# A dynamic convolution in front of a tanh-shrink layer: products in two tiles, softmax four superblocks ahead, one part of the products on VectorE, second sums from superblock 13 on

## The chip, the cores and the metric

The kernel runs on one core of a Trainium2 chip. A core has five engines that run beside each other, each with its own queue of instructions in order: TensorE (PE, matmuls; PEld is its loading of weights), VectorE (DVE), ScalarE (ACT), GpSimd (POOL) and SyncE (SP, which here only issues DMAs). GpSimd issues DMAs too. An instruction that waits for a semaphore holds up everything behind it on its engine. On-chip data lies in SBUF; matmuls write to PSUM, a small memory of eight banks. The metric is the time of one execution on the device in microseconds; lower is better.

## The reference

Cut to what is computed, with batch 8, sequence 4096, 192 channels, 8 heads of 24 channels and 7 taps, and a layer of 2048 hidden units:

```python
w = softmax(weight_gen, axis=-1)                 # per token, head: 7 weights
x_pad = np.concatenate([zeros(B, 6, D), x], axis=1)
x_unf = x_pad[:, idx, :].reshape(B, S, 7, 8, 24) # idx: the token and the six before it
out = np.einsum('bshk,bskhg->bshg', w, x_unf)    # sum over the 7 taps
h = out.reshape(B * S, D) @ w_in                 # 192 x 2048
g = h - np.tanh(h)
return g @ w_out                                 # 2048 x 192
```

All inputs and the output are float32.

## The kernel before

The 32768 tokens are cut into 32 superblocks (n = 0 to 31) of 1024 tokens, four to a sequence. Within one, partition p holds the eight tokens 8p to 8p + 7 (index j) and the six tokens ahead of them (the halo). A superblock goes through these steps:

- `load_x` and `load_wg` (SP's DMA queue) bring the tokens and the raw weights. Of x there are two tiles, of wg two. The first superblock of a sequence gets zeros over its halo by a further small DMA (L124).
- Softmax: `softmax_exp` on ScalarE (L147), two partial sums over the taps on VectorE (`softmax_sum`, L161), and at the end of a loop a reciprocal (L176) and a scaling (L207), both on VectorE with the reciprocals in a corner of a PSUM tile.
- `products`: GpSimd multiplies the tokens with the weights, one product tile per tap, all seven in one tile `pr` of 7 x 8 x 192 bfloat16 per partition (two such tiles, `ppool`). L236 is every such multiply; 1536 of its elements per partition are one tap.
- Sums by DMA: a DMA from GpSimd's queue that adds what it reads to what stands in its target (`dma_sum`, L214). The first sum adds taps 3, 4, 5 to 0, 1, 2, so that four tiles are left (6, 0, 1, 2). In the superblocks in `TWO_SUMS` a second sum adds 2 and 6 to 0 and 1, so that two are left. It's issued in `products` of the next superblock, behind that one's first multiply (`second_sum`). Superblocks 2 to 4 (`PART`) add only two taps and keep five tiles.
- Transposes (`conv_sums`, L311): matmuls with an identity turn the remaining tiles into channel-major form and add them up in PSUM; ScalarE copies the result out as `convT` (L337). Fewer tiles are fewer matmuls: each costs 48 (24 pairs) per superblock.
- `gemm1` (L354): 16 tiles f of hidden units, six matmuls each, in one of three PSUM tiles `ph`, which the transposes use as well. ScalarE computes the tanh (L367, `th`), VectorE the difference (L368, `gt`).
- `out_stream` (L389): the second matmul, as a stream of 128 small steps ("pairs") per superblock, running one superblock behind; ScalarE copies its results out (L408), and SP stores them (L412).

The order on every engine is written out by hand, in the order of the program. The loop over n has 16 steps f. At step f it issues `gemm1(n, f)`, and then what the plan names for this step: in `STEADY` and `FIRST`, `pairs` says how many steps of the output stream follow each f, `t2` and `t1` where the transposes of superblock n + 1 stand (f = 13 for two thirds of the channels and f = 14 for the last third), `sums` where VectorE's partial softmax sums stand, and `scale` where the scaling stands. At f = 1 come the exponential of n + 3 and `products(n + 2)`; at f = 7 the load of x for n + 3 (`X_AT`), held behind the last difference issued.

So loop n transposes n + 1, lets GpSimd work on n + 2, and makes the softmax of n + 3.

The softmax here doesn't subtract the row's maximum and nothing guards it: scores larger than these inputs give would overflow.

## Time and profile before

| what | before |
|---|---|
| time, median of 4 runs | 751.86 us (748.69 to 756.33) |
| time of the profiled execution | 751.58 us |
| its span, first to last instruction | 749.8 us |
| mean granted TensorE clock | 0.991 |
| L354 PE (gemm1), 3072 matmuls | 406.1 us busy |
| L389 PE (output stream), 7936 matmuls | 398.4 us busy |
| L311 PE (transposes), 2496 matmuls into pc | 49.9 us busy, 16.6 us idle before them |
| L368 DVE (difference), 512 | 603.3 us busy, mean 1219 ns |
| L367 ACT (tanh), 512 | 506.8 us busy, mean 1026 ns |
| L236 POOL (products), 95 | 629.8 us busy |
| L214 POOL (sums by DMA), 43 issues | 55.0 us busy |

"Busy" is the time in which at least one instruction of the group ran; instructions of one engine may overlap a little, so a sum of means can be over the busy time. "Idle before" is the time for which the engine stood still just ahead of the group, with the releaser that ended it. The lines by time give the start, the length, the engine, the line, the operation, the tile written and the tiles read, how many instructions are merged, and in brackets an idle time before it with its releaser. A DMA issue of GpSimd counts as busy for about 1.28 us; the data lands later.

### The profile page before, as it was taken

To read this page: it belongs to the slowest core of one execution; us is meant where nothing else is said; L and a number is where in the kernel's file an instruction comes from. 1 tells how busy PE (TensorE), PEld (TensorE's weight loads), DVE (VectorE), ACT (ScalarE), POOL (GpSimd) and SP (SyncE) were. 2 spreads that over 40 slices of the span, in tenths; PEclk is the share of its full clock that TensorE was granted. 3 is DMA by queue.
4 is the path that set the end of the run, shared out by engine and by line. 5 is a ranking of instruction groups with operands and counts; after the bars stand their busy time and mean duration, and the time that the engine had idled before them with its cause. 6 is when DMAs were issued, how large, how long until landed. Compare 5 with 4: busy or idle time off the path is not lost.

```text
span 749.8 us, 30497 instructions
## 1 busy us (share of the span) xinstructions
PE 723.4 (96%) x13928; PEld 564.5 (75%) x13928; DVE 664.6 (89%) x655; ACT 638.6 (85%) x872; POOL 668.7 (89%) x150
## 2 busy tenths in 40 slices
PE   3899999999999999999999999999999799999998
PEld 2477777777887777777777777777787577777777
DVE  7999889998889998999999999999989689998983
ACT  4888888888888888898989899898989588988883
POOL 7999999999999999999999999999999999999000
PEclk9899999999999999999999999999999899999999
DMA  8944536765655567785695787579668757673412
GB/s 233 245 104 114 171 115 167 192 181 126 178 154 170 171 177 158 200 192 167 193 233 143 185 209 179 170 198 210 166 173 184 186 153 183 184 178 84 112 44 87
DMA packets 32511, 124.99 MB, mean 167 GB/s; under 512 B 4495, under 2 KB 9343, under 8 KB 28414
## 3 DMA queue, kind: packets, MB, share of 16 engines
q0 software_dynamic: 17664, 46.01, 35.8%
q1 hardware_dynamic: 14718, 77.03, 27.6%
q8 instruction: 109, 1.79, 0.9%
q14 instruction: 20, 0.16, 0.1%
HBM read 54.52 MB, written 25.17 MB: 106 GB/s over the span
## 4 chain that ended last, share of the span: by engine, by line
PE 84%; DMA 5%; POOL 4%; DVE 4%; ACT 1%; issue 1%; SPq 0%; DVEq 0%; POOLq 0%
PE obank L389 39%; PE ph L354 39%; DMA pr<-pr 4%; PE pc L311 4%; POOL pr L236 4%; DVE gt L368 2%; PE po L432 1%; DVE pr L236 1%; DMA x_t<-zero 1%; ACT th L367 1%; ACT convT L337 0%; DVE wsm L207 0%; PE obank L311 0%; SPq L114 0%; POOL pr L214 0%
## 5 line engine op out<-in xcount | busy, mean ns | idle before, releaser
L368 DVE TENSOR_TENSOR gt<-ph,th 128x1024 bf16<-128x1024 f32 x512 | 603.3, 1219 | 65.3 <-ACT th L367 64.9
L236 POOL TENSOR_TENSOR pr<-x_t,wsm 128x3072 bf16<-128x3072 f32 (+3 forms) x95 | 629.8, 6830 | 7.0 <-PE obank L389 5.9
L367 ACT ACTIVATE th<-ph 128x1024 f32<-128x1024 f32 x512 | 506.8, 1026 | 70.5 <-PE ph L354 66.2
L354 PE MATMUL ph<-convT,w_in 64*128 64x512 bf16 x3072 | 406.1, 379 | 5.9 <-DVE gt L368 3.5
L389 PEld LDWEIGHTS <-gt 64*128 64x128 bf16 x7936 | 351.8, 94 | 73.7 <-issue 11.1
L389 PE MATMUL obank<-w_out,gt 64*128 64x192 bf16 x7936 | 398.4, 243 | 0.2 <-issue 0.2
L354 PEld LDWEIGHTS <-w_in 64*128 64x128 bf16 x3072 | 169.9, 95 | 83.6 <-issue 12.0
L408 ACT ACTIVATE out_sb<-obank 128x192 f32<-128x192 f32 x248 | 82.3, 332 | 12.7 <-PE obank L389 10.1
L214 POOL DMA_DIRECT2D pr<-pr x43 | 55.0, 1280 | 20.3 <-DMA pr<-pr 10.7
L311 PEld LDWEIGHTS <-pr 64*128 64x128 bf16 x2664 | 51.0, 101 | 24.1 <-POOL pr L236 10.4
L311 PE MATMUL pc<-ident,pr 64*128 64x64 bf16 x2496 | 49.9, 193 | 16.6 <-POOL pr L236 10.3
L337 ACT ACTIVATE convT<-pc 128x1024 bf16<-128x1024 f32 (+1 forms) x62 | 50.5, 816 | 6.8 <-PE pc L311 6.3
L161 DVE TENSOR_REDUCE zsum<-e_t 128x32 f32<-128x224 f32 (+1 forms) x61 | 23.7, 388 | 2.8 <-ACT e_t L147 2.8
L147 ACT ACTIVATE e_t<-wg_t 128x448 f32<-128x448 f32 x32 | 18.2, 569 | 7.6 <-DMA wg_t<-in_weight_gen_dram 7.6
L207 DVE TENSOR_TENSOR wsm<-e_t,pc 128x448 f32<-128x448 f32 x28 | 17.4, 621 | 3.3 <-DVE pc L176 0.5
L176 DVE RECIPROCAL pc<-zsum 128x64 f32<-128x64 f32 x28 | 15.4, 551 | 0.0
L432 PE MATMUL po<-w_out,gt 64*128 64x192 bf16 x256 | 11.2, 243 | 0.0
L236 DVE TENSOR_TENSOR pr<-x_t,obank 128x1536 bf16<-128x1536 f32 (+4 forms) x8 | 10.4, 1350 | 0.8 <-ACT wsm L199 0.6
L432 PEld LDWEIGHTS <-gt 64*128 64x128 bf16 x256 | 10.8, 93 | 0.0
L446 DVE TENSOR_TENSOR out_sb<-po,ot 128x192 f32<-128x192 f32 x8 | 2.9, 358 | 9.0 <-ACT ot L445 9.0
L445 ACT ACTIVATE ot<-po 128x192 f32<-128x192 f32 x8 | 2.6, 331 | 7.3 <-PE po L432 7.3
L467 POOL DMA_DIRECT2D w_in<-in_moe_w_in_dram x4 | 2.4, 627 | 2.8 <-ACT e_t L147 2.8
(19 smaller groups left out, 18.3 us busy)
## 6 DMA issues: line engine op xcount, KB each, us to landing
x_t<-in_x_dram SPq DMA_DIRECT2D x31, 1344.0 KB, 6.0
pr<-pr POOLq DMA_DIRECT2D x27, 1152.0 KB, 9.9
out_dram<-out_sb SPq DMA_DIRECT2D x31, 768.0 KB, 3.8
pr<-pr POOLq DMA_DIRECT2D x16, 768.0 KB, 6.7
wg_t<-in_weight_gen_dram SPq DMA_DIRECT2D x32, 224.0 KB, 6.8
x_t<-in_x_dram SPq DMA_DIRECT2D x1, 768.0 KB
w_out<-in_moe_w_out_dram POOLq DMA_DIRECT2D x1, 768.0 KB, 9.6
out_dram<-out_sb SPq DMA_DIRECT2D x4, 192.0 KB, 4.0
```

What stands on the lines that cost most here:

```text
L147: last_exp[0] = nc.scalar.activation(out=e_t[:].rearrange("p j h k -> p (j h k)"), in_=wg_t[:].rearrange("p j h k -> p (j h k)"), func=ACT ...
L161: nc.vector.reduce_sum(out=zsum_of[n][:, j0 * H : j1 * H], in_=e_of[n][:, j0:j1].rearrange("p j h k -> p (j h) k"), axis=AX.X,)
L214: nc.gpsimd.dma_start(out=pr[:, k0:k1].rearrange("p k j d -> p k (j d)"), in_=pr[:, src0:src1:step].rearrange("p k j d -> p k (j d)"), acc ...
L236: return eng.tensor_mul(pr[:, k0:k1, j0:j1, :].rearrange("p k j (h g) -> p k (j h) g", h=H), bass.AP(tensor=x_v.tensor, offset=x_v.offset ...
L311: nc.tensor.matmul(pc[r][:, col : col + R] if home else pc[:, r, col : col + R], lhsT=prods[c][gi][r * R : (r + 1) * R, 2 * j : 2 * j + 2] ...
L337: last_conv[0] = nc.scalar.activation(out=out, in_=pc[:, :, 0:cols].rearrange("p r (cj t) -> p r cj t", t=R), func=ACT.Copy,)
L354: nc.tensor.matmul(ph[:, r, :], lhsT=w_in[r * R : (r + 1) * R, c, f * P : (f + 1) * P], rhs=convT[r * R : (r + 1) * R, c, :], start=(c == ...
L367: last_act[0] = nc.scalar.activation(out=th[:], in_=ph_f, func=ACT.Tanh)
L368: last_sub[0] = nc.vector.tensor_sub(gt[:], ph_f, th[:])
L389: mm = nc.tensor.matmul(po[:, 0:D], lhsT=g_of[n][f][r * R : (r + 1) * R, col : col + P], rhs=w_out[r * R : (r + 1) * R, f, :], start=(r == ...
L408: last_act[0] = nc.scalar.activation(out=out_sb[:, j, :], in_=po[:, 0:D], func=ACT.Copy)
L432: nc.tensor.matmul(po[:, r, 0:D], lhsT=g_of[n][f][r * R : (r + 1) * R, col : col + P], rhs=w_out[r * R : (r + 1) * R, f, :], start=(f == 0 ...
```

## The change

- The products lie in two tiles: `pa` with taps 0 to 3 (three buffers) and `pb` with taps 4 to 6 (one buffer). GpSimd multiplies taps 0 and 1, taps 2 and 3, and taps 4 to 6. The first sum adds all of `pb` to taps 0 to 2 and stands behind the last multiply; the second sum adds taps 2 and 3 to 0 and 1 and stands in the next superblock's products behind its second multiply.
- For superblocks from 4 on (`HELP`), GpSimd's first multiply leaves out the last of the eight tokens; VectorE makes these two taps of that token at f = 3 of the loop, by a copy of 16 weights to the PSUM tile of that f and a multiply of 384 elements. `products` returns `rest`, which holds this and the remaining GpSimd work and is called at f = 3.
- `TWO_SUMS` holds all superblocks from 13 on (19 instead of 13).
- The softmax runs four superblocks ahead from loop 4 on (loop 4 makes two); the exponential is computed in place, with three tiles of raw weights and four of softmax results.
- `load_x` of n + 3 stands at f = 1, held behind GpSimd's first multiply of n + 2. The first superblock of a sequence is loaded without its halo in the first partition, in three DMAs and the zeros.
- The product of superblock 1 is cut differently, with two tiles in place of `pb` out of the output's pool. The plans `STEADY` differ in `pairs` and `sums`.

```diff
-    TWO_SUMS = tuple([n for n in range(13,NTOT) if n%3])
-    SUM_FIRST = tuple(range(5,32))
+    KA, KH = 4, 2
+    TWO_SUMS = (13, 14, 15, 16, 17, 18, 19, 20, 21, 22, 23, 24, 25, 26, 27, 28, 29, 30, 31)
+    AHEAD = 4
+    HELP_AT = 3
...
-    wgpool = ctx.enter_context(tc.tile_pool(name="wgpool", bufs=2))
-    ppool = ctx.enter_context(tc.tile_pool(name="ppool", bufs=2))
+    wgpool = ctx.enter_context(tc.tile_pool(name="wgpool", bufs=3))
+    papool = ctx.enter_context(tc.tile_pool(name="papool", bufs=3))
+    pbpool = ctx.enter_context(tc.tile_pool(name="pbpool", bufs=1))
+    wspool = ctx.enter_context(tc.tile_pool(name="wspool", bufs=4))
...
-            mul(nc.gpsimd, 0, 2)
-            second_sum(n - 1)
-            mul(nc.gpsimd, 2, 6)
-            if n in SUM_FIRST:
-                dma_sum(pr, 0, 3, 3, 6)
-            mul(nc.gpsimd, 6, K)
...
+        x_after[n + 1] = mul(nc.gpsimd, 0, KH, 0, J - 1 if n in HELP else J)
+        mul(nc.gpsimd, KH, KA)
+        second_sum(n - 1)
+
+        def rest(ph=None):
+            if n in HELP:
+
+                w = ph[:, 0, 0 : KH * H].rearrange("p (k h) -> p k h", k=KH)
+                nc.vector.tensor_copy(w, wsm[:, J - 1].rearrange("p h k -> p k h")[:, 0:KH])
+                nc.vector.tensor_mul(
+                    pa[:, 0:KH, J - 1, :].rearrange("p k (h g) -> p k h g", h=H),
...
+                    w.rearrange("p k (h o) -> p k h o", o=1).to_broadcast([P, KH, H, G]),
+                )
+            if n in PART:
+                dma_sum(pa[:, 0:2], pa[:, 2:4])
+            mul(nc.gpsimd, KA, K)
...
+                dma_sum(pa[:, 0:3], pb[:, 0:3])
...
     def second_sum(n):
 
         if n in to_sum:
-            dma_sum(to_sum.pop(n), 0, 2, 2, K, 4)
+            pa = to_sum.pop(n)
+            dma_sum(pa[:, 0:2], pa[:, 2:4])
...
-        taps=[(V, 0, 1, 0, J), (V, 1, 2, 0, J), (G_, 2, 5, 0, J), (G_, 5, 7, 0, J)],
+        taps=[(V, 0, 1, 0, J), (V, 1, 2, 0, J), (G_, 4, 6, 0, J), (G_, 6, 7, 0, J), (G_, 2, 4, 0, J)],
...
-    STEADY = dict(pairs=(4, 12, 0, 16, 0, 16, 0, 16, 0, 6, 10, 6, 10, 8, 8, 16), t1=(14, 8), t2=(13, 0), scale=14, sums=(2, 5))
+    STEADY = dict(pairs=(5, 11, 0, 16, 4, 12, 6, 10, 0, 6, 10, 8, 8, 8, 8, 16), t1=(14, 8), t2=(13, 0), scale=14, sums=(1, 13))
...
+        soft = [m for m in (n + 3,) * (n <= AHEAD) + (n + 4,) * (n >= AHEAD) if m < NTOT]
         for f in range(NFT):
-            gemm1(n, f)
+            ph = gemm1(n, f)
...
-            if f == X_AT and n + 3 < NTOT:
-                load_x(n + 3, last_sub[0])
+            if f == (9 if n == 1 else HELP_AT) and n + 2 < NTOT:
+                rest(ph)
+            if f == (9 if n == 1 else 1):
+                emit_x(n + 3)
+                if soft and n != AHEAD and soft[0] + 1 < NTOT and n > 1:
+                    load_wg(soft[0] + 1)
```

`emit_x(m)` calls `load_x(m, x_after[m])`.

## The prediction, made before the change was run

> **What bounds the kernel now.** I read the page's busy shares first, then the chain of waits, then single loops of the steady part, then the one place where TensorE stands still.
>
> ```profile
> PE 723.4 (96%) x13928; PEld 564.5 (75%) x13928; DVE 664.6 (89%) x655; ACT 638.6 (85%) x872; POOL 668.7 (89%) x150
> PE 84%; DMA 5%; POOL 4%; DVE 4%; ACT 1%; issue 1%; SPq 0%; DVEq 0%; POOLq 0%
> ```
>
> TensorE is busy for 96% and carries 84% of the chain; the 5% of DMA and 4% of POOL in it are one place, shown below. VectorE and GpSimd are at 89% each, so a cut on TensorE is worth something only while both still keep up. Two whole loops, one whose transposes take four product tiles per token block (n = 5 to 12 and every third later), one with two (both sums made):
>
> ```profile
> 130.10:152.50 22.40, 22.40 (x454) 17.61 (x451) 20.36 (x21) 19.83 (x27) 22.10 (x5) 1.00 0.60 162
> 505.69:527.41 21.72, 21.72 (x403) 16.83 (x400) 20.29 (x20) 19.59 (x28) 21.42 (x6) 1.00 0.86 213
> ```
>
> The columns are the stretch, its length, then PE, PEld, DVE, ACT and POOL busy, granted clock, DMA share. TensorE has no gap at full clock in either: 22.40 us is its own length with four tiles, 21.72 us with two. VectorE leaves 2.04 and 1.43 us free. GpSimd's own pace is in its timeline:
>
> ```profile
> 112.11 1.28 POOL L214 DMA_DIRECT2D pr<-pr  x1 [0.30 <-POOL pr L236]
> 112.93 19.99 POOL L236 TENSOR_TENSOR pr<-x_t,wsm 128x1536 bf16<-128x1536 f32 x3
> 133.22 1.30 POOL L214 DMA_DIRECT2D pr<-pr  x1 [0.30 <-POOL pr L236]
> ...
> 373.04 1.28 POOL L214 DMA_DIRECT2D pr<-pr  x1 [0.30 <-POOL pr L236]
> 373.86 8.97 POOL L236 TENSOR_TENSOR pr<-x_t,wsm 128x1536 bf16<-128x1536 f32 x2
> 382.75 1.26 POOL L214 DMA_DIRECT2D pr<-pr  x1
> 383.53 11.59 POOL L236 TENSOR_TENSOR pr<-x_t,wsm 128x6144 bf16<-128x6144 f32 x1
> 395.42 1.28 POOL L214 DMA_DIRECT2D pr<-pr  x1 [0.30 <-POOL pr L236]
> ```
>
> From one first sum to the next: 133.22 - 112.11 = 21.11 us with one sum, 395.42 - 373.04 = 22.38 us with two. So GpSimd gains 1.3 us on TensorE per one-sum superblock and loses 0.7 us or more per two-sum one (more where it also waits for the first sum to land, up to 1.53 us). The debt comes due here:
>
> ```profile
> 584.95 1.22 POOL L214 DMA_DIRECT2D pr<-pr  x1 [1.28 <-DMA pr<-pr]
> ```
> ```profile
> 596.33 1.04 PE L311 MATMUL pc<-ident,pr 64*128 64x64 bf16 x32 [5.58 <-DMA pr<-pr]
> 597.16 1.49 PE L389 MATMUL obank<-w_out,gt 64*128 64x192 bf16 x16
> 598.42 1.51 PE L354 MATMUL ph<-convT,w_in 64*128 64x512 bf16 x6
> 599.70 1.16 PE L389 MATMUL obank<-w_out,gt 64*128 64x192 bf16 x16
> 600.68 0.41 PE L311 MATMUL pc<-ident,pr 64*128 64x64 bf16 x16
> ```
>
> The second sum of superblock 26, issued at 584.95, is awaited by its transposes: TensorE idles 5.58 us. The four groups after it take 4.35 us from start to start (596.33 to 600.68), where the same four took 2.44 us one loop of this kind earlier (502.58 to 505.02). The stall costs 5.58 + 1.91 = 7.5 us.
>
> **The change, part by part.**
>
> Transposes. Superblocks 15, 18, 21, 24, 27 and 30 go from four tiles to two. The two transposes of a superblock take 0.93 + 0.46 us with four (starts 123.95 to 124.88, 126.85 to 127.31) and 0.47 + 0.23 us with two (502.58 to 503.05, 505.02 to 505.25): 0.69 us less, six times, 4.1 us. All of it lies on the path, as TensorE has no gap there.
>
> GpSimd. The multiplies become 2688, 3072 and 4608 wide instead of 3072, 6144 and 1536: three as before, 384 fewer elements. Rows of the ramp give 2.90, 5.62 and 8.33 us for 1536, 3072 and 4608, so 1.77 ns per element, and 0.68 us less per superblock from n = 4. The new paces are 20.43 us with one sum and 21.70 us with two, against 22.40 and 21.72 of TensorE: the debt stops growing. The wait before the second sum goes too: it now stands behind two multiplies, 11.8 us after the first sum's issue (0.8 + 0.45 + 4.94 + 5.58, the 0.45 being what a multiply loses while a sum is issued), and in before it could start 10.4 to 11.4 us after it wherever it waited.
>
> GpSimd's head start. The second sum stands one multiply later than before, so superblock n needs its first sum issued about 18.5 us before its transposes (11.8 plus a median 6.7 to land). The ramp reaches the first sum of n = 5 at 113.9 us (112.11; +0.2 for product 1 cut in three; -0.68 for n = 4; +2.25 because the sum now comes behind the last tap: 8.33 + 5.58 + 4.94 against 11.02 + 5.58 after the previous tap group). Its transposes start at 123.95 with a tile that needs no sum, and that sum landed 9.8 us after issue: 0 to 1 us of stall, I take 0.3. By n = 13 GpSimd is at 113.9 + 8 x 20.43 = 277.3; the transposes are due at 280.93 + 22.40 = 303.3; that leaves 7.5 us, kept to the end at equal pace. The 7.5 us stall goes, and what is late next is nothing of GpSimd's.
>
> The single second product tile (the three last taps of n + 1 wait for the sum of n to land, 8.8 to 12.1 us, 11.8 covered): at most 0.3 us of GpSimd, inside the head start. Softmax four ahead and three first tiles remove the waits "POOL pr <- PE obank" (5.9 us over five places, all off TensorE's path): nothing for the end, if they came back they'd cost head start.
>
> SP's queue. The load of x(n+3) moves to f = 1 and waits for GpSimd's first multiply of n + 2. Behind it stand one weight load and one store of the output. In the ramp that multiply ends near 79 us, so the weights of 6 land near 86.5, about when their exponential is due in loop 3 (84.1 + 2.8): 0 to 1 us, I take 0.2. Later the multiply is done before the queue gets there. The extra loads at a sequence start replace one load and an overwrite; they land long before use.
>
> VectorE. 28 superblocks (n = 4 to 31, in loops 2 to 29) get a copy of 16 elements and a multiply of 384, right behind the subtraction of f = 3, in order before that of f = 4. The multiply has a row: 128x384 took 547 ns. The copy has none: reciprocals of 32 and 64 elements took 343 and 551 ns, so their fixed part is 135 ns, and products of 192 and 384 (356, 547 ns) give 165 ns; I take 0.18 us, bounds 0.13 and 0.34. Two waits of VectorE on itself, as between reciprocal and scale (0.10 us): together 0.85 us after the 0.08 by which neighbours overlap, between 0.75 and 1.1. VectorE then needs 21.14 of 21.72 us. Who waits: the next subtraction, and the matmuls of f = 6, which take the PSUM tile that the copy writes. In the loop at 507 us the subtraction of f = 3 ends at 514.4, about 0.3 earlier once the partial sum at f = 2 has moved to f = 1 (there 0.26 us were idle); the help ends at 515.0 and the matmuls of f = 6 start at 515.09. The later subtractions are met the same way, since the partial sum of f = 5 goes to f = 13 (0.60 us idle behind it) and the pairs now spread the matmuls of f = 4 to 7. So it just fits, with under 0.1 us to spare; I take 0.05 us per loop, 1.4 us. Loop 4 makes two softmaxes: 0.75 + 0.55 + 0.62 more on VectorE against about 1.2 us free, 0.6 us.
>
> A rule that speaks against it: the Trainium skill, "GPSIMD Engine Reference", Key points, says that GpSimd shares its SBUF interfaces with VectorE and suffers from VectorE instructions with two SBUF inputs. No VectorE row here has two SBUF inputs beside a GpSimd multiply, and the new one reads its weights from PSUM, so by the rule nothing is added. Were it to count all the same, GpSimd would stand still for the 0.55 us of that row, 10 us over the last 19 superblocks, 3 us of it past the head start (an estimate).
>
> Sum: 749.8 - 4.1 - 7.5 + 0.3 + 0.2 + 1.4 + 0.6 = 740.7 (the 0.2 of product 1 is covered: its transposes start 1.3 us after its last multiply). The profiled execution's time is 1.8 us above its span (751.58), and the median 0.3 above that: 742.8. The small costs may be zero (740.3). I forecast 742.
>
> **The rivals.**
>
> VectorE's help is dearer than it fits (1.1 to 1.3 us instead of 0.85): TensorE waits 0.2 to 0.4 us in each of 28 loops, 747 to 752. For: the margin worked out above is under 0.1 us. Against: VectorE's total still leaves time, and three tiles of tanh and PSUM take up jitter.
>
> GpSimd gains nothing: the 2688 multiply, cut out of each tap's row, costs as much as 3072 (5.62 us). Then the first sum of 13 comes at 114.6 + 8 x 21.11 = 283.5, the head start is 0.6 us, and 18 superblocks lose 0.66 us each: 11.3 us of stall, 753. Against: the rows at four widths lie on one line.
>
> Slower: the help lands wholly on TensorE's path, as VectorE's one in-order queue holds the subtraction of f = 4 and the PSUM tile of f = 6. Below about 0.9 us it hides; from 1.6 us on TensorE loses 0.7 us or more in 28 loops, 20 us: 760 and above. For: no row shows such a pair beside GpSimd's wide multiplies, and it waits twice for VectorE itself. Against: the 384 row.
>
> That the change does not do what it says: the instruction order shows both sums of 13 to 31, so this is excluded; TensorE's odd gap such as the 0.96 us at 290, put down to "issue", may stay.
>
> **How the numbers follow.** The four runs of before spread over 1.0% (748.69 to 756.33), so 1% is what can be told from no change: 744.3 and 759.4. Forecast 0.57 (738 to 746, a tenth of it above 744.3), dear help 0.14, GpSimd unchanged 0.09, slower 0.17, other small stalls 0.03. Faster 0.51, same 0.32, slower 0.17. The range 738 to 758 leaves out the slower case and a little below.
>
> **What would show it.** Right: no TensorE wait over 1 us on a sum past 300 us; loops of 21.7 us from 300 to 700; GpSimd at 20.4 and 21.7 us from first sum to first sum; the copy and multiply 0.7 to 0.9 us together. Wrong: waits of the f = 6 or f = 7 matmuls on VectorE in every loop (second or fourth case), or the 2688 multiply near 5.6 us (third). A TensorE wait near 124 us over 1 us would mean that the single second tile or the later sum of the ramp costs more than I gave it.

## The result, and the profile after

| what | before | after |
|---|---|---|
| time, median | 753.04 us (64 runs, 744.84 to 756.36) | 755.59 us (43 runs, 753.00 to 760.48) |
| profiled execution, its span | 751.58, 749.8 us | 756.84, 755.1 us |

The ratio on record is 1.005, with a 95% interval of 1.0037 to 1.0062 (that of the two medians is 1.003): a little slower, and inside the 1% that the prediction counted as no change. The forecast of 742 us is missed by 14 us. Between the spans of the profiled executions, the prediction's sum had 9.1 us of gain (749.8 to 740.7); 5.3 us were lost.

First the page of the changed kernel, busy shares and chain:

```profile
PE 723.6 (96%) x13640; PEld 560.2 (74%) x13640; DVE 685.4 (91%) x711; ACT 640.7 (85%) x872; POOL 656.9 (87%) x157
PE 93%; DVE 3%; issue 2%; ACT 1%; DMA 0%
```

TensorE issues 288 matmuls fewer and is as long busy as before (723.6 to 723.4 us). The chain has lost its 5% of DMA and its 4% of GpSimd, as forecast, and "issue" has gone from 1% to 2%. Whole stretches tell where the time went; each line is the stretch and its length, the busy time of PE, PEld, DVE, ACT and POOL, the granted clock, the DMA share and GB/s. Before, from the transposes of superblock 4 to those of 13, and from there to those of 31:

```profile
101.20:304.70 203.50, 202.54 (x4058) 161.16 (x4056) 183.39 (x181) 178.97 (x243) 199.09 (x38) 1.00 0.62 165
304.70:708.20 403.50, 397.62 (x7491) 309.80 (x7489) 363.76 (x355) 354.13 (x485) 373.57 (x83) 0.99 0.71 177
```

After, the same work:

```profile
102.00:316.30 214.30, 204.06 (x4059) 161.94 (x4057) 191.57 (x203) 180.24 (x245) 202.54 (x42) 1.00 0.70 172
316.30:712.70 396.40, 394.55 (x7204) 304.68 (x7202) 375.04 (x386) 354.65 (x484) 357.31 (x85) 1.00 0.78 188
```

From superblock 13 on the change gains 7.1 us. Before that, where it takes nothing from TensorE, the same instructions take 10.8 us longer, 9.3 of them with TensorE idle (214.30 - 204.06 against 203.50 - 202.54). With 0.8 us lost at each end that is the 5.3 us. What TensorE waits for in the early part is in its timeline; the brackets hold the idle time before the line and its releaser:

```profile
107.00 0.45 PE L336 MATMUL pc<-ident,pb 64*128 64x64 bf16 x19 [1.57 <-issue]
...
133.45 0.57 PE L415 MATMUL obank<-w_out,gt 64*128 64x192 bf16 x9 [1.55 <-issue]
...
155.70 0.32 PE L415 MATMUL obank<-w_out,gt 64*128 64x192 bf16 x3 [1.65 <-issue]
...
227.86 0.57 PE L415 MATMUL obank<-w_out,gt 64*128 64x192 bf16 x9 [2.42 <-issue]
...
250.10 0.32 PE L415 MATMUL obank<-w_out,gt 64*128 64x192 bf16 x3 [1.37 <-issue]
...
276.38 0.57 PE L415 MATMUL obank<-w_out,gt 64*128 64x192 bf16 x9 [1.42 <-issue]
```

Six stretches, 10.0 us, each in or shortly after the transposes of superblocks 4, 5, 6, 9, 10 and 11. No semaphore event ends them: their operands are there. A stretch breaks off in the middle of a run of equal matmuls (the 16 of one group stand as 7 and 9). GpSimd's own lines show that it is not late:

```profile
136.66 1.30 POOL L219 DMA_DIRECT2D pa<-pb  x1 [0.30 <-POOL pb L253]
...
157.11 1.28 POOL L219 DMA_DIRECT2D pa<-pb  x1 [0.30 <-POOL pb L253]
...
385.87 9.33 POOL L253 TENSOR_TENSOR pb<-x_t,wsm 128x4608 bf16<-128x4608 f32 x1
395.50 1.28 POOL L219 DMA_DIRECT2D pa<-pb  x1 [0.30 <-POOL pb L253]
396.32 11.01 POOL L253 TENSOR_TENSOR pa<-x_t,wsm 128x2688 bf16<-128x2688 f32 x2
406.79 1.72 POOL L219 DMA_DIRECT2D pa<-pa  x1
407.57 9.32 POOL L253 TENSOR_TENSOR pb<-x_t,wsm 128x4608 bf16<-128x4608 f32 x1
417.28 1.28 POOL L219 DMA_DIRECT2D pa<-pb  x1 [0.39 <-POOL pb L253]
```

395.50 to 417.28 is 21.78 us from first sum to first sum with two sums (21.70 forecast); with one sum it is 20.45 (136.66 to 157.11; 20.43 forecast). No transposes wait for a sum any more.

**What an "issue" stretch is.** The page's queues list one that is neither a sum nor a load of data; after, and its row before:

```profile
q0 software_dynamic: 19296, 50.73, 39.1%
q1 hardware_dynamic: 15040, 77.00, 29.9%
q8 instruction: 106, 1.74, 0.9%
```
```profile
q8 instruction: 109, 1.79, 0.9%
```

The columns are packets, MB and share of the engines' time. 1.74 MB in 106 packets are 16.4 KB each; and TensorE has 2 x 13640 = 27280 instructions (matmuls and weight loads), 256 times 106.6. Before, the row says 109 and its 27856 instructions are 256 times 108.8. So each packet is a block of 256 instructions of TensorE, which comes through the same DMA engines as the data. Counted in TensorE's instructions, block i starts to load when TensorE is about 182 past 256 i if the DMA engines are free, and later if they are busy. From the DMA records of all 18 kernels (1668 such loads between 80 and 720 us), by how far TensorE was past 256 i when the load began (its few waits for semaphores counted too), with the longest pause between two TensorE starts around it or in the 1.5 us behind it:

```
past 256 i     loads   with a pause over 0.45 us   mean pause
under 380       1570     51                        0.2 us
380 to 399        32      8                        0.4
400 to 419        26     24                        1.3
420 to 444        26     26                        1.9
445 to 449        14     14                        2.9
over 449           0
```

No load ever began later than 449 past its boundary: there TensorE has nothing left and stands still. The records show it directly. Of the 179 pauses of over 0.6 us between two TensorE starts in these traces, 105 begin at exactly this count, 449 past a boundary, and each of them ends 1.0 to 1.7 us after the block's load has ended; the other 74 are waits for other engines or for DMAs, with their releaser in the profile. In the changed kernel all six stretches are among the 105. A load that begins later than 400 nearly always comes with a pause (64 of 66), as it takes about 1 us itself; around small matmuls one that begins earlier can too. In the changed kernel there are six loads later than 400, and they are the six stretches; in before there is one, which is the 0.96 us at 290 that the prediction left as "may stay". How soon 400 is reached depends on what TensorE runs. The 218 instructions from 182 to 400 last up to 7.0 us in the steady loop of before and only 3.0 us around the transposes with their four tiles, whose matmuls are small. The transposes of superblocks 5 to 12 start at the same count in both kernels (121 or 249 past a boundary, by turns), and the 218 instructions there last 3.4 and 3.6 us. What differs is the delay of the loads, counted from TensorE's 182nd instruction past the boundary: between 100 and 315 us it is over 2.5 us for 11 of 34 loads before, 19 of 32 after. In that time GpSimd's DMAs hold 34% of the engines in both, SP's 28% before and 35% after, for 22.6 and 24.2 MB.

Nine of these loads are due at the transposes of superblocks 4 to 12, and since the count is the same, they are the same nine blocks in both kernels. Their delays in us, what the DMA engines were moving in the 0.5 us from when each was due (SP's transfers, a sum, or nothing), and the stretch that followed:

```
superblock        4      5      6      7      8      9      10     11     12
before, delay    1.8    0.7    2.6    0.6    2.9    0.8    2.3    0.7    2.8
  moving         SP     SP     SP     SP     SP     SP     SP     SP     SP
after, delay     3.6    3.9    4.5    0.7    0.8    4.7    4.3    3.9    2.4
  moving         SP     SP     SP     -      -      sum    sum    SP     sum
  stretch        1.57   1.55   1.65   -      -      2.42   1.37   1.42   -
```

The six loads with over 3.5 us are the six stretches, and before has none over 2.9. The lengths can be worked out too (an estimate): in the loops of before, the 267 instructions from 182 to 449 last 4.5 us for the odd superblocks and 5.0 for the even ones, and 4.1 for superblock 4; a load takes some 1.0 us and TensorE goes on some 1.4 us after its end; so a delay over 2.1, 2.6 or 1.7 us stops TensorE, for as long as it is over. For superblocks 4, 5, 6, 9, 10 and 11 that gives 1.9, 1.8, 1.9, 2.6, 1.7 and 1.8 us; from start to start of TensorE's instructions the pauses are 1.8, 1.8, 1.9, 2.7, 1.6 and 1.7.

### The profile page after: what moved, and what is told of

Read it like the earlier page. It is cut to its first block, busy times and chain, and to the rows that moved or that the text cites. A ratio compares the mean times of both kernels' runs of the same rounds, so it can differ in the third digit from the quotient of the medians.

```text
span 755.1 us, 30078 instructions
## 1 busy us (share of the span) xinstructions
PE 723.6 (96%) x13640; PEld 560.2 (74%) x13640; DVE 685.4 (91%) x711; ACT 640.7 (85%) x872; POOL 656.9 (87%) x157
## 3 DMA queue, kind: packets, MB, share of 16 engines
q0 software_dynamic: 19296, 50.73, 39.1%
q8 instruction: 106, 1.74, 0.9%
## 4 chain that ended last, share of the span: by engine, by line
PE 93%; DVE 3%; issue 2%; ACT 1%; DMA 0%
PE obank L415 44%; PE ph L379 44%; PE pc L336 4%; PE po L458 1%; DVE gt L393 1%; DVE pa L253 1%; ACT th L392 1%; DVE pb L253 0%; DMA wg_t<-in_weight_gen_dram 0%; DVE obank L194 0%; DVE zsum L166 0%; DVE wsm L212 0%; DVE obank L212 0%; ACT convT L354 0%; ACT wg_t L152 0%
## 5 line engine op out<-in xcount | busy, mean ns | idle before, releaser
L253 POOL TENSOR_TENSOR pa<-x_t,wsm 128x3072 bf16<-128x3072 f32 (+2 forms) x63 | 342.1, 5671 | 0.1
L253 POOL TENSOR_TENSOR pb<-x_t,wsm 128x4608 bf16<-128x4608 f32 (+2 forms) x33 | 284.6, 8624 | 3.1 <-PE pc L336 2.7
L219 POOL DMA_DIRECT2D pa<-pb x27 | 34.7, 1284 | 20.0 <-DVE pa L287 13.2
L336 PEld LDWEIGHTS <-pa 64*128 64x128 bf16 x2016 | 41.3, 101 | 7.0 <-DVE pa L253 1.0
L219 POOL DMA_DIRECT2D pa<-pa x22 | 35.9, 1630 | 8.7 <-DMA pa<-pb 7.8
L336 PE MATMUL pc<-ident,pa 64*128 64x64 bf16 x1920 | 40.6, 192 | 1.3 <-POOL pa L253 0.7
L166 DVE TENSOR_REDUCE zsum<-wg_t 128x32 f32<-128x224 f32 (+1 forms) x61 | 23.7, 388 | 2.8 <-ACT wg_t L152 2.8
L152 ACT ACTIVATE wg_t<-wg_t 128x448 f32<-128x448 f32 x32 | 18.2, 570 | 7.4 <-DMA wg_t<-in_weight_gen_dram 7.4
L212 DVE TENSOR_TENSOR wsm<-wg_t,pc 128x448 f32<-128x448 f32 x28 | 17.3, 621 | 2.7
L181 DVE RECIPROCAL pc<-zsum 128x64 f32<-128x64 f32 x28 | 15.5, 552 | 3.8 <-ACT convT L362 3.7
L287 DVE TENSOR_TENSOR pa<-x_t,ph 128x384 bf16<-128x384 f32 x28 | 15.5, 554 | 1.2
```

Source lines behind the costliest of these rows:

```text
L152: last_exp[0] = nc.scalar.activation(out=wg_t[:].rearrange("p j h k -> p (j h k)"), in_=wg_t[:].rearrange("p j h k -> p (j h k)"), func=AC ...
L166: nc.vector.reduce_sum(out=zsum_of[n][:, j0 * H : j1 * H], in_=e_of[n][:, j0:j1].rearrange("p j h k -> p (j h) k"), axis=AX.X,)
L219: return nc.gpsimd.dma_start(out=out.rearrange("p k j d -> p k (j d)"), in_=in_.rearrange("p k j d -> p k (j d)"), accum_op=mybir.AluOpTyp ...
L253: return eng.tensor_mul(prod(k0, k1)[:, :, j0:j1].rearrange("p k j (h g) -> p k (j h) g", h=H), bass.AP(tensor=x_v.tensor, offset=x_v.offs ...
L336: nc.tensor.matmul(pc[r][:, col : col + R] if home else pc[:, r, col : col + R], lhsT=prods[c][gi][r * R : (r + 1) * R, 2 * j : 2 * j + 2] ...
```

## The experiments

Each kernel was timed beside the kernel before; the ratios are to it, with their 95% intervals. The expectations stand with the theories as they were when each was written; where letters are used, F and F2 are forms of the theory of late instructions.

### Where x is loaded, and VectorE's help

x_at_f7: the changed kernel, x at the place that it had before, and the raw weights behind it.

```diff
-            if f == (9 if n == 1 else 1):
-                emit_x(n + 3)
+            if f == 7 and n + 3 < NTOT:
+                load_x(n + 3, last_sub[0])
...
```

> The changed kernel with the loads of x and of the raw weights back at f = 7, x held behind the last difference, as before the change; all else as changed. Theory F (the new place of the x load puts its traffic beside the first sum's, around the transposes, and TensorE's own instructions then come late: the six idle stretches of 1.4 to 2.4 us put down to 'issue' between 105 and 277 us): four or more of the six go, and the time falls by 6 to 12 us, to 743 to 749. Theory V (the gaps come with VectorE's help and the new pair plan, not with the load): the gaps stay, within 2 us of the changed kernel.

780.32 us, 1.0336 (1.0269 to 1.0402). Five stretches of over 1 us are still there between 150 and 300 us (1.72, 1.15, 2.34, 1.30 and 1.55 us), so x's new place is not enough to explain them; that theory fell. At the nine loads of the table all nine now meet SP's transfers (one a sum as well), and five of them wait 3.6 to 4.8 us. And x comes too late for the faster GpSimd. Its waits (total, times, longest), and one of those that they cause on TensorE:

```profile
POOL pa L253 <- DMA x_t<-in_x_dram: 29.3, 11, 6.2
```
```profile
460.58 1.04 PE L336 MATMUL pc<-ident,pa 64*128 64x64 bf16 x32 [7.54 <-DMA pa<-pa]
```

x_at_f15: x of n + 4 at the end of loop n, behind the last difference.

```diff
...
+            if f == NFT - 1 and n + 4 < NTOT:
+                load_x(n + 4, last_sub[0])
```

> The changed kernel with x of n + 4 loaded at f = 15 of loop n, just behind the transposes, held behind the last difference (its traffic then lies about 4 to 7 us into the next loop, far from that loop's transposes). Theory F: all six gaps go, 741 to 746. Theory V: the gaps stay, within 2 us of the changed kernel.

783.08 us, 1.0404 (1.0364 to 1.0444). No "issue" stretch of 1 us between 105 and 520 us, but GpSimd waits 33.8 us in all for its own first sums, which land later, and TensorE waits for sums (5.01 us at 130.8, 7.01 at 335). At the nine loads the longest delay is 3.3 us. It removes the stretches, as expected, and shows nothing of what they cost, as something dearer takes their place: 741 to 746 us had been expected.

no_help: the changed kernel with `HELP = ()`.

> The changed kernel without VectorE's part of the products: GpSimd makes all taps of all tokens. Theory F: GpSimd's pace is 21.1 and 22.4 us, the x load follows it, so gaps of 1.4 us and more stay between 105 and 300 us, perhaps at other superblocks; the loops with two tiles fall from 21.86 to 21.72 us until GpSimd's lead is used up, then TensorE waits for second sums, 5 to 11 us in all: 750 to 760. Theory V: no gaps before 300 us, TensorE reaches superblock 13 some 12 us earlier, and then the same waits for second sums.

757.93 us, 1.0057 (1.0017 to 1.0097): as the changed kernel. The stretches are there without VectorE's help (2.25 us at 132, 1.91 at 155, 2.44 at 273), so the help does not cause them. The waits for second sums that were expected (5 to 11 us) did not come. Its two-tile loops take 21.82 us, against 21.86 with the help and 21.72 before: of the 0.14 us only 0.04 is the help.

before_x_f12: the kernel before with `X_AT = 12`.

> The kernel before with its x load moved from f = 7 to f = 12, so that its traffic lies at the transposes. Theory F: new gaps of 1 us and more put down to 'issue' at the transposes, 5 to 20 us slower than before. Theory V: no such gaps, since help and plan are those of before; at most 3 us slower (GpSimd gets x later).

772.94 us, 1.0265 (1.0214 to 1.0316). The new stretches that were expected did not come: there is no late instruction load at all. With x at its new place all nine loads are due while nothing moves, and none waits over 0.9 us. Instead there are seven waits on sums, 15.8 us. x later costs GpSimd its head start in before too.

### The transposes spread out, and x left out

spread and before_spread: the output steps of f = 13 and 14 stand between the matmuls of the transposes instead of behind them, from loop 4 on, in either kernel.

```diff
...
-        for _ in conv_sums(n, (chunks,), pcs):
-            pass
+        for i, _ in enumerate(conv_sums(n, (chunks,), pcs), 1):
+            if per and i % per == 0:
+                out_pairs(1)
```

> The changed kernel with the transposes spread: the 16 steps of the output stream that stand at f = 13 and f = 14 are put between the matmuls of the two transposes, one after every 8 or 4 of them, from loop 4 on; the same matmuls, DMAs and other engines' work. The theory is now F2: any DMA burst (first sum, or x with weights and store behind it) keeps TensorE's 16 KB instruction loads waiting for 3 to 5 us; TensorE has some 240 instructions in hand, which last 5 us and more in the output stream but only 2 to 3 us in the transposes, so it runs dry only where a late load meets the transposes. F2: the stretches of 1.4 us and more put down to 'issue' between 105 and 300 us go (the one in superblock 4's transposes at 105 may stay), 742 to 747. Rival D (the stalls are decided by the amount of DMA traffic alone, wherever the transposes stand): the gaps stay or move into the stream, 751 to 758.

768.60 us, 1.0192 (1.0144 to 1.0241). The stretches were expected to go; one of the six did, four shrink little (1.29, 0.72, 2.00, 1.15 us at 136, 158, 231, 280), and that in the transposes of superblock 4, which might stay, grows (2.15 at 109). And the order has a price of its own in every loop, as the transposes hold their PSUM tile for longer:

```profile
367.79 0.21 PE L336 MATMUL pc<-ident,pa 64*128 64x64 bf16 x2 [0.45 <-DVE gt L393]
```

> The kernel before with its transposes spread in the same way. F2: its one such gap (0.96 us at 290 us, together 1.4 us) goes, nothing else changes, as its wait for the second sum of superblock 26 stays: 748 to 752. D: no change, or slower where the spreading itself costs; a cost of spreading would show here as loops over 22.40 and 21.72 us.

759.58 us, 1.0086 (1.0059 to 1.0112), with the same wait, 0.60 us in the two-tile loops. The pair does not decide on the stretches.

x_left_out: the changed kernel without the loads of x from superblock 8 on. The products of those superblocks use the tokens of earlier ones, so that part of the output is not computed.

```diff
...
-        if m < NTOT:
+        if m >= 8:
+            x_of[m] = kept[m % 2]
+        elif m < NTOT:
             load_x(m, x_after.pop(m, None))
+            kept[m % 2] = x_of[m]
```

> The changed kernel without the loads of x from superblock 8 on (their products are made from the tokens of 6 and 7, so this part of the result is left out); raw weights, sums and stores stay. F2: from loop 5 on the gaps that lay in SP's traffic (153 and 274 us) go, those in a first sum's (225 and 248 us) may stay: 744 to 751. If loads were late for a reason other than DMA traffic (theory V, VectorE or the plan), the gaps stay all the same: 752 to 757.

748.79 us, 0.994 (0.9916 to 0.9963). The median delay of an instruction load falls from 2.4 to 1.0 us, and of the stretches only these two over 1 us are left, the first of them before the first load that is left out:

```profile
131.41 0.57 PE L415 MATMUL obank<-w_out,gt 64*128 64x192 bf16 x9 [1.96 <-issue]
...
268.30 0.57 PE L415 MATMUL obank<-w_out,gt 64*128 64x192 bf16 x9 [1.88 <-issue]
```

So the traffic of the data is what delays the instructions, and with most of the traffic of x gone, 7 us come back (755.59 to 748.79). The 1668 loads of all traces say the same: the median delay is 0.6 us for the 452 that were due while data held under a tenth of the DMA engines, and 3.2 us for the 1035 that were due while it held over nine tenths.

### Which superblocks make second sums

two_from_9: the changed kernel with `TWO_SUMS = tuple(range(9, NTOT))`.

> The changed kernel with both sums from superblock 9 on instead of 13: four more second sums (more DMA traffic), and transposes of two tiles instead of four in 9 to 12. In the trace of the changed kernel TensorE takes 281 instructions in the 4 us from the start of four-tile transposes, 212 with two tiles, 132 in the stream, and ran dry wherever some 240 were used up while a load of instructions was on its way. F2: the gaps of 2.4, 1.4 and 1.4 us at 228, 250 and 276 us fall under 0.6 us each; with 4 x 0.69 us of transposes saved the time falls by 6 to 10 us, 746 to 750. Rival D (DMA traffic alone decides): the gaps stay or grow, and only the 2.8 us come off: 752 to 757.

751.70 us, 0.999 (0.996 to 1.0019). There is more DMA traffic (53.87 MB in GpSimd's queue instead of 50.73), but fewer instructions in the transposes of 9 to 12, and the stretches at 228, 250 and 276 are gone. Those in superblocks 5 and 6, still with four tiles, stay:

```profile
131.09 0.57 PE L415 MATMUL obank<-w_out,gt 64*128 64x192 bf16 x9 [1.45 <-issue]
...
153.62 0.32 PE L415 MATMUL obank<-w_out,gt 64*128 64x192 bf16 x3 [1.93 <-issue]
```

Between 420 and 585 us there are new ones of 0.5 to 1.35 us, so not all of the 8.0 us that the four superblocks might bring (2.8 of matmuls, 5.2 of stretches) arrive.

two_as_before: the changed kernel with before's list, `[n for n in range(13, NTOT) if n % 3]`.

> The changed kernel with the second sums of before (not in 15, 18, 21, 24, 27, 30): six second sums fewer, six four-tile transposes more. F2: beside 4.1 us for the transposes, gaps of 1 us and more appear in two or more of those six superblocks, where none were over 0.51 us from 316 us on: 760 to 768. D: less traffic, the small gaps after 316 us shrink, 757 to 760.

764.41 us, 1.0149 (1.011 to 1.0188). Besides the early stretches (2.40 us at 226, 1.65 at 275) there is a late one at superblock 15, which has four tiles again: 1.43 us at 364. A second one stands under another name, at superblock 21:

```profile
496.77 0.84 PE L415 MATMUL obank<-w_out,gt 64*128 64x192 bf16 x16 [1.34 <-ACT convT L362]
```

The profile puts these 1.34 us down to ScalarE, but here too TensorE stops 449 past a boundary and goes on 1.4 us after the load has ended. The six superblocks cost 8.8 us in all, twice the 4.1 of their own TensorE time; these two stretches are the largest part of the rest.

before_two_13: the kernel before with `TWO_SUMS = tuple(range(13, NTOT))`.

> The kernel before with second sums in all superblocks from 13 on and nothing else: what that part does without VectorE's help and the two tiles. By GpSimd's pace (22.4 us and the wait for the first sum to land, 22.4 to 23.5 us, against TensorE's 21.72) its lead of about 4 us at 13 is gone after three or four superblocks, and TensorE then waits 0.7 to 1.8 us in each of some 15: 755 to 768, waits on a second sum (DMA) and no large 'issue' gaps. If instead GpSimd kept up, 748 or less.

767.65 us, 1.0184 (1.0146 to 1.0223). The second sums alone are not to be had in before: GpSimd falls behind and TensorE stands still, twice for over 6 us, where 0.7 to 1.8 us in each of some 15 superblocks had been expected.

```profile
444.63 1.04 PE L311 MATMUL pc<-ident,pr 64*128 64x64 bf16 x32 [6.68 <-DMA pr<-pr]
...
631.18 1.04 PE L311 MATMUL pc<-ident,pr 64*128 64x64 bf16 x32 [7.00 <-DMA pr<-pr]
```

So the second sums need other parts of the change to keep up; in the changed kernel no transposes wait for them.

store_first: the changed kernel with `emit_x` at f = 2 instead of 1, so that the store of the output goes ahead of x in SP's queue.

> The changed kernel with the load of x and of the weights at f = 2 instead of 1, so that in SP's queue the store of the output stands ahead of them and isn't held by x's wait for GpSimd. F2 with the burst of x, weights and store as its cause: the gaps at 133, 155 and 276 us, which lay in SP's traffic, shrink by half or go, 747 to 752. If x's own traffic beside a first sum is enough: gaps as before, 753 to 758.

763.26 us, 1.013 (1.0087 to 1.0173). Of the three stretches that were expected to shrink by half or go, the one at 133 us goes and those at 155 and 276 stay (1.45 and 1.26 us); the one at 107 us shrinks to 0.64 us. But GpSimd waits 22.3 us for x (8 times), and TensorE then waits for sums.

### The count of instructions alone

So far the place in the loop and the count of instructions went together. Here only the count moves: matmuls of the identity into a tile that nobody reads, before the first transposes, where TensorE is idle for 9 us. One is a weight load and a matmul, so 26 of them are 52 instructions and 90 are 180.

```diff
+    dum = psum_h.tile([P, 2, HT], FP32, name="dum", tag="ph")
+    for _ in range(26):
+        nc.tensor.matmul(dum[:, 0, 0:R], lhsT=ident[0:R, :], rhs=ident[0:R, 0:R], start=True, stop=True)
     conv(0, (0, 1), (2,))
```

> The changed kernel with 52 more TensorE instructions (26 loads and 26 matmuls of the identity into a tile that nobody reads) before its first transposes, where TensorE stands idle for 9 us; all the rest stays. Instruction-load theory: the trace's 16 KB loads of TensorE's instructions stand at every 256th instruction, and a load that comes more than about 400 instructions after its boundary leaves TensorE without any. In the steady loops of before, 218 instructions after the usual place of such a load (boundary + 182) are used up in 3.2 us if the transposes start 124 past a boundary (superblocks 5, 7, 9, 11 of the changed kernel) and in 3.6 us if 252 past it (6, 8, 10, 12). 52 more put these at 176 and 48, where they last 3.0 and 4.5 us. So the stretches of over 1 us at superblocks 6 and 10 should go, those at 5, 9 and 11 stay or grow to 2 to 3 us; about 751 to 756 us. Rival (TensorE waits for something tied to the work, not to the count of its instructions): stretches of 1.4 to 2.4 us at the same superblocks 4, 5, 6, 9, 10, 11 as in the changed kernel, and 755 us.

> The changed kernel with 180 more TensorE instructions (90 loads and 90 matmuls of the identity into a tile that nobody reads) before its first transposes. Instruction-load theory: the odd superblocks come to 48 (4.5 us for 218 instructions), the even ones to 176 (3.0 us). So the stretches at superblocks 5, 9 and 11 should go, and those at 6 and 10 stay or grow; 4 comes to 127 (3.0 us instead of 3.6) and stays; perhaps new ones at 8 or 12. About 751 to 756 us. Rival (tied to the work): the same list of superblocks as in the changed kernel, 755 us. The two shifts together decide, as each theory names different superblocks.

770.54 us, 1.0213 (1.0174 to 1.0252), and 767.20 us, 1.0173 (1.0131 to 1.0214): 12 to 15 us over the changed kernel, for work that the idle time of the start hides. The "issue" stretches of 0.4 us and more, in us, at superblocks 4 to 13, by the superblock whose transposes they follow (or break off, as at 107 us):

```
superblock    4     5     6     7    8     9     10    11    12    13
after        1.57  1.55  1.65   -    -    2.42  1.37  1.42   -     -
shift_52     2.86  2.64  0.58   -   0.46  3.09  1.30  2.38  1.11  1.38
shift_180    3.67   -     -     -   2.75  1.94  2.18  1.19  2.41   -
```

With 52, 5, 9 and 11 have the long ones, where the 218 instructions last 3.0 us, and that of 6 shrinks to a third; with 180, 4 keeps its own, 5 has none, and 8, 10 and 12 get long ones. That is as the theory said. Not as it said: the stretches of 10 (with 52) and of 9 and 11 (with 180) shrink and don't go, so the 4.5 us that the 218 instructions last there are not always enough; and superblocks 12 and 13 of shift_52 were not expected at all. The rival, a wait tied to the work, would have left the list and the time alone, and falls. In the timeline of shift_52 TensorE stops after three of the six matmuls of one gemm1 group, fed by a convT that was made a whole loop earlier:

```profile
135.44 0.65 PE L336 MATMUL pc<-ident,pa 64*128 64x64 bf16 x32
135.91 0.59 PE L379 MATMUL ph<-convT,w_in 64*128 64x512 bf16 x3
139.14 0.59 PE L379 MATMUL ph<-convT,w_in 64*128 64x512 bf16 x3 [2.64 <-issue]
```

These stretches cost more than their length. The stretch of time behind one of shift_52, and behind the longest of the changed kernel, in the columns of the windows above:

```profile
235.59:239.60 4.01, 4.01 (x43) 3.52 (x44) 1.22 (x1) 1.35 (x2) 4.01 (x2) 0.57 0.84 160
```
```profile
227.86:231.80 3.94, 3.94 (x63) 3.24 (x64) 1.62 (x2) 2.98 (x6) 3.94 (x2) 1.00 1.03 266
```

The granted clock is 0.57 in the one, 1.00 in the other. In both shifts all four stretches that stop gemm1 are followed by 3.8 to 4.0 us at 0.56 to 0.64, some 1.6 us lost each. For shift_52 the sum closes: "issue" grows from 12.0 to 20.6 us, four times 1.6 us make 6.4, together 15.0 of the 15.5 us in the span.

two9_shift_84: the kernel of two_from_9 with 42 such matmuls.

> The kernel of two_from_9 (second sums from superblock 9 on) with 84 more TensorE instructions before its first transposes, put there so that superblock 4 comes to 31 past a boundary (4.3 us for 218 instructions instead of 3.6), 5 to 207 (3.6 instead of 3.2) and 6 to 79 (4.1 instead of 3.6). Instruction-load theory: the stretches at 131 (1.45) and 154 us (1.93) shrink to under 1 us each, and what comes after 400 us moves to other superblocks; 746 to 751 us, 1 to 4 us below two_from_9. Rival (tied to the work): both stretches stay at 1.4 to 2 us, 751 us.

751.39 us, 0.998 (0.9959 to 1.0001). The list changes (1.76, 1.75 and 1.29 us at 111, 132 and 154, then 1.13 to 0.64 up to 272, and nothing of note later), the sum hardly. The expected gain did not come, and the stretches at 132 and 154 did not fall under 1 us, as they should have.

before_shift_52 and before_shift_180: the same two shifts of the kernel before.

> The kernel before with 52 more TensorE instructions (26 loads and 26 matmuls of the identity into a tile that nobody reads) before its first transposes. Up to superblock 12 before and the changed kernel start their transposes at the same count past a boundary (123 and 251), so the count can't be what parts them there: the loads come 0.6 to 3.0 us after their usual place in before (superblocks 5 to 12, near the transposes) and up to 4.7 us in the changed kernel. Theory (the change made the loads later): with 176 past a boundary 218 instructions last 3.0 us, which before's delays hardly reach; at most one or two stretches over 1 us, and within 4 us of before, 749 to 756 us. Rival (before has a lucky count, and any other costs it as much as the changed kernel): stretches of 2 to 3 us in superblocks 5, 7, 9, 11 and 765 us or more.

> The kernel before with 180 more TensorE instructions in the same place. Theory (the change made the loads later): at most one or two stretches over 1 us, 749 to 757 us; the even superblocks (8 had a delay of 2.9 us, 12 of 2.8 us) are the nearest to one. Rival (lucky count): stretches of 2 to 3 us in superblocks 4, 6, 8, 10, 12 and 765 us or more.

753.19 us, 0.9985 (0.9959 to 1.001), and 748.27 us, 0.9939 (0.9914 to 0.9964). No load later than 400 in either, one stretch over 0.5 us (0.83). So before does not live off a lucky count: it bears both shifts, as its loads come in time (median delay 1.4 us in both, 2.6 and 2.5 us in the shifted changed kernels). The wait for a second sum moves by the shift: in the first it is 5.47 us at 664. The second is the fastest complete kernel of this study. Its profile has no stretch at 290 us, and its only wait of this kind is:

```profile
527.13 0.65 PE L311 MATMUL pc<-ident,pr 64*128 64x64 bf16 x32 [2.03 <-DMA pr<-pr]
```

## Why the prediction was wrong, by its steps

- **The stall of superblock 26 (-7.5 us): right.** No transposes wait for a sum in the changed kernel, and no_help shows that even the new tiles without the help suffice for that. The size is that of one trace: in the two shifts of before the wait is 5.47 and 2.03 us.
- **GpSimd's paces (20.43 and 21.70 us): right**, 20.45 and 21.78. They also leave no room for the contention with VectorE that the prediction weighed: of its 0.55 us per superblock no more than 0.08 is seen. The rival of this step, a 2688 multiply at the price of 3072, is refuted by the same rows.
- **The transposes (-4.1 us): right as a term.** The six superblocks have two tiles. With the stall it makes -11.6 us from superblock 13 on; measured are -7.1. The difference is in the next two points.
- **VectorE's help (1.4 us): the price right, the term too small.** Copy and multiply take 0.19 and 0.55 us, as worked out (0.18 and 0.55):

```profile
394.09 0.19 DVE L286 COPY ph<-wsm 128x16 f32<-128x16 f32 x1
394.32 0.55 DVE L287 TENSOR_TENSOR pa<-x_t,ph 128x384 bf16<-128x384 f32 x1
```

  But a two-tile loop is 0.14 us longer than before, 18 x 0.14 = 2.5 us, and by no_help 0.10 of it is not the help's. The new order of the pairs and partial sums may be behind it; it was not tried alone. The other 2 us from 13 on are five stretches of 0.23 to 0.51 us (1.7 us together).
- **The ramp (0.3 + 0.2 + 0.6 us): a little low.** The first sum of superblock 5 came at 116.24 instead of 113.9 us and nobody waited for it. What made it late is the single second product tile, for which the prediction had at most 0.3 us: the transposes of superblock 4 still read it, held up themselves by the stretch at 107 us, and GpSimd waited for them (total, times, longest):

```profile
POOL pb L253 <- PE pc L336: 2.7, 1, 2.7
```

  The transposes of superblock 4 are 0.8 us late, 0.40 of it a wait of TensorE for ScalarE's copy of the output in loop 3.
- **SP's queue (x moved to f = 1, with "one weight load and one store of the output" behind it, taken at 0.2 us in the ramp and at nothing later): the step that failed, and the direction with it.** It asked only whose data would come late, and the step on GpSimd's pace likewise asked nothing of where the sums' transfers would come to stand. The transfers also delay TensorE's instructions, and no term of the prediction's sum stands for that: the loops of superblocks 5 to 12 were taken to stay at 22.40 us. It is the 10.8 us between superblocks 4 and 13: six stretches of 10.0 us in all, four of them at loads that met SP's transfers and two at loads that met a sum. The prediction had met one such stretch, the 0.96 us at 290, and let it stand as "may stay" without asking what it was.
- **The rivals.** Neither the dear help, nor the slow 2688 multiply, nor the help on the path came. The signs listed for them were the right ones to look for, and they are absent; that the time came out among theirs, and inside the range of 738 to 758, is luck.

That the stretches are lacking instructions is shown, by the count at which TensorE stops in every run and by the two shifts. That traffic makes the loads late is shown by x_left_out and by the delays of all loads. What the change did in superblocks 4 to 12 is in the table of the nine loads: SP's transfers keep four of them waiting for 3.6 to 4.5 us (at most 2.9 us before), and two wait 4.3 and 4.7 us for a sum, while before none of the nine met one. Over all loads between 100 and 315 us the median is 3.6 us for those that meet a sum (3.5 before), and 3.7 for those that meet SP's transfers (1.8 before). Which edit of the change moved them there is not settled. SP's transfers take 35% of the engines instead of 28%. At the first of the stretches x, the weights and the store of the output leave SP's queue within 1.3 us; before, the store left 14 us after x:

```profile
99.39 0.33 SPq L119 DMA_DIRECT2D x_t<-in_x_dram  x1
99.77 0.43 SPq L105 DMA_DIRECT2D wg_t<-in_weight_gen_dram  x1
100.25 0.42 SPq L438 DMA_DIRECT2D out_dram<-out_sb  x1
100.71 0.63 SPq L105 DMA_DIRECT2D wg_t<-in_weight_gen_dram  x1
```
```profile
96.32 0.33 SPq L114 DMA_DIRECT2D x_t<-in_x_dram  x1
96.69 0.43 SPq L100 DMA_DIRECT2D wg_t<-in_weight_gen_dram  x1
110.46 0.34 SPq L412 DMA_DIRECT2D out_dram<-out_sb  x1
```

But x_at_f7, with SP's share back at 29%, keeps stretches, and there GpSimd's times moved as well. It may be that GpSimd's faster pace carries the sums, and x which waits for it, through the transposes' place in the loop; that is argued, not shown.

## What to carry to other kernels

A stretch that the profile calls "issue", in the middle of equal matmuls whose operands are there, can be an engine out of instructions: look in the DMA queues for the instruction loads, divide the instructions by their packets, and see how far past its boundary each load began. Where a stage of many small matmuls meets full DMA engines, an edit that moves transfers can have this price, and fewer instructions there can be worth more than their own length (two_from_9 gained some 4 us on the changed kernel, 2.8 of them the length of the matmuls saved). A change of 1% is worth repeating with the count of instructions shifted by a few matmuls in idle time: here that alone moved the changed kernel by 15 us and the kernel before by -5.

## What the runs showed of the hardware that was not expected

- TensorE's instructions come in loads of 16.4 KB (256 instructions) through the DMA engines that move the data. A load begins about 182 instructions past the boundary when the DMA engines are free; the median delay from there was 1.2 us before and 2.4 after, and one reached 8.4 us.
- TensorE never got further than 449 past a boundary without the next load, 267 instructions after the load's usual place, and went on 1.0 to 1.7 us after the load's end (105 pauses). Around transposes with four tiles these 267 instructions last 4.5 or 5.0 us in before's loops.
- After some stretches the granted clock falls to 0.56 to 0.66 for about 4 us. Of the 60 "issue" stretches of 1 us and more in the 18 traces it does so after all six that are longer than 2.5 us, after 8 of the 15 between 1.9 and 2.5 us, and after none of the 39 shorter ones; it happens behind stops of gemm1 and of the output stream. What decides between 1.9 and 2.5 us was not tried. The 1.91 us that the prediction counts behind before's wait of 5.58 us at 596 are of the same kind: the granted clock is 0.54 there.
- The profile merges most of these waits under "issue", since no semaphore ends them (one stood under ScalarE), and the 0.9% share of the instruction queue looks like nothing: it's the delay that costs, not the bytes.
